# Attention row sums as four concurrent 32-column tiles, and the PSUM banks regrouped, in a beacon-attention plus GEGLU kernel

## The chip, the cores and the metric

The kernel runs on one core of one Trainium2 chip. The metric is the device time of one execution in microseconds (us). Every kernel was timed in several rounds beside the kernel before on the same chip, and fast runs are compared with fast runs. The profile that is quoted is one profiled execution. Its span runs from the first to the last instruction, and it is some 2 us shorter than the time.

Engines: PE is TensorE doing matmuls, PEld is TensorE loading weights, DVE is VectorE, ACT is ScalarE, POOL is GpSimd. PSUM is the memory that the matmuls of this program write to; the program cuts it into banks of 512 columns. The granted clock is TensorE's clock as a share of full speed.

A trace can lack a few per cent of the matmul records. "Start to start" is the time between the starts of two matmuls that follow each other.

## The reference

The sizes are batch 8, 8 heads, 576 queries, 576 + 16 keys (the "beacon" keys come first and everybody sees them), head dimension 64. The attention output, 4608 tokens of 512 values, goes through a GEGLU block with 1536 hidden values.

```python
k_all = np.concatenate([beacon_k, k], axis=2)          # 16 + 576 keys
v_all = np.concatenate([beacon_v, v], axis=2)
scores = scale * np.matmul(q, k_all.transpose(0, 1, 3, 2))
scores = np.where(causal, -1000000000.0, scores)       # beacons never masked
a = np.exp(scores - scores.max(-1, keepdims=True))
a /= a.sum(-1, keepdims=True) + 1e-09                  # the row sums of this case
x = np.matmul(a, v_all)                                # -> (4608, 512)
g = x @ w_gate
gelu = 0.5 * g * (1.0 + erf(g * inv_sqrt2))
return gelu * (x @ w_val) @ w_out
```

## The kernel before

The program goes through the eight batch entries. Each has an *attention stage* over four head pairs, called heads 0 to 3 here and in the prediction, and then a *gate stage* over 512 tokens. A head pair goes like this: scores on TensorE, exp on ScalarE (four instructions), masks (on GpSimd; in batch entry 0 on VectorE), then `attend`, which makes the value product X and the row sums Z, and `normalize`, which makes X/Z and writes it to `xT_sb`. Between them stand the out-projection matmuls of the token chunk before, the calls `o(n)`. They are the filler of the attention stage.

`attend` makes the row sums with a matrix of ones of 64 columns. One head of the pair lands in partitions 0 to 63, the other in 64 to 127, and each row sum is written 64 times over:

```python
for w, (ps, base, split) in enumerate(x_of[i]):        # w = 0: X, w = 1: Z
    for q0, q1 in ((S_LO[t], split), (max(split, S_LO[t]), S)):
        # ... (cut)
        for hi in range(2):
            mm(ps[64 * hi : 64 * hi + 64, base + q0 : base + q1],
               ones[0:kr, :] if w else v_sb[0:kr, t, 2 * m + hi, :],
               expT[0:kr, hi, e0 : e0 + q1 - q0], ...)
```

`normalize` does not take the reciprocal of all 128 x 576 copies. It transposes blocks of 32 x 32, takes the reciprocal of one column of each block, and transposes back with a broadcast. In batch entry 0 ScalarE does it with Ln and Exp instead (`by_act`).

```python
if by_act:
    act(ln_sb, z_ps, ACT.Ln)
    # ... (cut)
    act(rec_sb, ln_sb, ACT.Exp, scale=-1.0)
else:
    if not direct:
        act(x_sb, x_ps, ACT.Copy)
    keep(nc.vector.transpose(zT_sb, z_ps))
    keep(nc.vector.reciprocal(r_sb, zT_sb...[:, :, 0:1]))
    keep(nc.vector.transpose(rec_sb..., r_sb.to_broadcast([P, S // 32, 32])))
keep(nc.vector.tensor_tensor(out=xT_sb[:, m, b * S : (b + 1) * S], in0=x_sb, in1=rec_sb, op=ALU.mult))
```

The order of one batch entry, and of its first gate tile:

```python
o(6); ab(0); o(10); cd(0); o(8)        # ab, cd: scores and exps, two halves
for m in range(1, NPAIR):
    ab(m); av(m - 1); cd(m)            # av: attend and normalize
    o(6 if m < NPAIR - 1 else 5)
av(3, direct=True)
o(7)
for fi in range(F_TILES):
    gate_val(b, fi, kk_late=fi == 0)   # first tile: the two matmuls that need head 3 come last
    # ... (cut: after the first tile, GpSimd issues the loads of entry b + 2)
```

The eight matmuls of the first gate tile are sorted so that the seventh is the first that needs head 3. That *seventh gate matmul* is where an attention stage ends for TensorE, and most of this document is about it.

The softmax here doesn't subtract the row's maximum and nothing guards it: scores larger than these inputs give would overflow.

## Time and profile before

| before | |
|---|---|
| time, median of 3 fast runs | 398.17 us (397.83 to 398.93) |
| span of the profiled run | 396.2 us |
| TensorE busy | 382.3 us (97%) |
| seventh gate matmul after the last xT, all eight stages | 0.05 us |
| normalisation, first transpose to end of xT (29 of them) | 2.68 to 2.69 us |
| X and Z of one head pair on TensorE | 1.56 us |
| start of the last score matmul after the one before, entries 2 to 7 | 334 to 339 ns, against 204 ns without a wait |

The first line of the profile page's part 1 gives the busy time and share of each engine, and the first line of part 4 the chain of waits, shared out among the engines. Both say TensorE. The third line is from the list of waits: what waited for what, total us, times, longest.

```profile
PE 382.3 (97%) x3046; PEld 185.9 (47%) x3046; DVE 190.5 (48%) x304; ACT 202.2 (51%) x280; POOL 156.3 (39%) x277
...
PE 79%; DMA 8%; POOL 3%; DVE 3%; ACT 3%; issue 2%; SPq 2%; POOLq 0%; ACTq 0%
...
PE gv_ps L155 <- DVE xT_sb L312: 0.8, 1, 0.8
```

VectorE seems to be of no weight: busy 48%, 3% of the chain. The end of a stage shows something else. Here are the VectorE timeline of the kernel before at the end of batch entry 2, and under it the TensorE timeline at the same place. The columns are start, duration, engine, line, operation, tiles, shapes, count.

```profile
114.70 0.78 DVE L304 STREAM_TRANSPOSE zT_sb<-x_ps 128x576 f32<-128x576 f32 x1 [0.74 <-ACT x_sb L158]
115.52 0.27 DVE L305 RECIPROCAL r_sb<-zT_sb 128x18 f32<-128x18 f32 x1
115.82 0.78 DVE L307 STREAM_TRANSPOSE rec_sb<-r_sb 128x576 f32<-128x576 f32 x1
116.63 0.76 DVE L312 TENSOR_TENSOR xT_sb<-x_sb,rec_sb 128x576 bf16<-128x576 f32 x1
117.31 0.78 DVE L304 STREAM_TRANSPOSE zT_sb<-x_ps 128x576 f32<-128x576 f32 x1
118.12 0.27 DVE L305 RECIPROCAL r_sb<-zT_sb 128x18 f32<-128x18 f32 x1
118.42 0.78 DVE L307 STREAM_TRANSPOSE rec_sb<-r_sb 128x576 f32<-128x576 f32 x1
119.23 0.76 DVE L312 TENSOR_TENSOR xT_sb<-x_ps,rec_sb 128x576 bf16<-128x576 f32 x1
```

```profile
118.64 0.81 PE L155 MATMUL gv_ps<-xT_sb,wg_sb 128*128 128x512 bf16 x3
119.28 0.81 PE L155 MATMUL gv_ps<-xT_sb,wv_sb 128*128 128x512 bf16 x3
120.04 0.38 PE L155 MATMUL gv_ps<-xT_sb,wg_sb 128*128 128x512 bf16 x1
```

The chains of heads 2 and 3 stand one behind the other on VectorE without a gap. The last ends at 119.23 + 0.76 = 119.99, and the seventh gate matmul starts at 120.04. TensorE's starts are 216 ns apart there and this one comes 327 ns after the sixth: a wait of only 0.11 us. The program is tuned so that VectorE and TensorE arrive at the same moment. VectorE has no slack, and in entries 1 to 7 two whole normalisations of each stage lie on that path.

### The profile page before, as it was taken

How to read it: one execution, taken by the hardware profiler on the slowest of the kernel's cores; microseconds unless marked ns; L12 is line 12 of the kernel's file. 1: busy time of each engine (PE TensorE's matmuls, PEld its weight loads, DVE VectorE, ACT ScalarE, POOL GpSimd, SP SyncE). 2: the span in 40 equal slices, each digit the busy share in tenths (PEclk: the TensorE clock that was granted, in tenths of full speed). 3: DMA queues.
4: the chain of work that ended last, by engine and by line, in shares of the span. 5: the costliest groups of instructions: out<-in, count | busy, mean ns of one | idle time of the engine just before them, and what ended most of it. 6: DMA issues, size and time to landing. Idle time of an engine off the chain costs nothing.

```text
span 396.2 us, 7413 instructions
## 1 busy us (share of the span) xinstructions
PE 382.3 (97%) x3046; PEld 185.9 (47%) x3046; DVE 190.5 (48%) x304; ACT 202.2 (51%) x280; POOL 156.3 (39%) x277
## 2 busy tenths in 40 slices
PE   3889999999999999999999999999999999999996
PEld 2464545544454445444544455444544455444442
DVE  1393654844375327642673338433754266332332
ACT  2775258634873379336843586347823793332210
POOL 8722395780369124931486047803400240000000
PEclk9999999999999999999999999999999999999999
DMA  7999998699129930996099915991032010000012
GB/s 91 180 206 204 175 132 97 68 169 121 55 36 156 141 79 30 120 156 84 29 107 162 89 55 57 163 137 58 28 89 59 34 45 32 0 0 29 28 53 106
DMA packets 139154, 36.24 MB, mean 91 GB/s; under 512 B 126832, under 2 KB 134512, under 8 KB 139120
## 3 DMA queue, kind: packets, MB, share of 16 engines
q0 software_dynamic: 103984, 19.14, 64.4%
q1 hardware_dynamic: 35136, 16.62, 19.3%
q8 instruction: 24, 0.39, 0.4%
q14 instruction: 10, 0.08, 0.1%
HBM read 38.27 MB, written 9.44 MB: 120 GB/s over the span
## 4 chain that ended last, share of the span: by engine, by line
PE 79%; DMA 8%; POOL 3%; DVE 3%; ACT 3%; issue 2%; SPq 2%; POOLq 0%; ACTq 0%
PE gv_ps L155 36%; PE o_ps L155 23%; PE x_ps L155 11%; PE s_ps L155 8%; DMA qkT<-k_sb_94 3%; DMA v_sb_98<-in_beacon_v_dram 2%; SPq L196 2%; ACT expT L158 2%; DMA k_sb_97<-in_k_dram 2%; POOL k_sb_97 L109 1%; PE t_ps L167 1%; DVE qkT L178 1%; POOL q_sb_96 L109 1%; PE w_ps L155 1%; DMA kb<-in_beacon_k_dram 1%
## 5 line engine op out<-in xcount | busy, mean ns | idle before, releaser
L158 ACT ACTIVATE ge_sb<-gv_ps 128x512 bf16<-128x512 f32 x108 | 64.5, 597 | 150.7 <-PE gv_ps L155 150.7
L340 DVE TENSOR_TENSOR hT_sb<-gv_ps,ge_sb 128x512 bf16<-128x512 f32 x108 | 74.7, 692 | 116.0 <-ACT ge_sb L158 116.0
L158 ACT ACTIVATE expT<-s_ps 128x1024 bf16<-128x1024 f32 (+3 forms) x128 | 103.9, 870 | 25.8 <-PE s_ps L155 25.7
L155 PE MATMUL gv_ps<-xT_sb,wg_sb 128*128 128x512 bf16 x432 | 112.2, 379 | 0.8 <-DVE xT_sb L312 0.8
L155 PE MATMUL gv_ps<-xT_sb,wv_sb 128*128 128x512 bf16 x432 | 112.2, 379 | 0.0
L238 POOL TENSOR_SCALAR_AFFINE_SELECT expT<-expT 128x256 bf16<-128x256 bf16 (+2 forms) x140 | 52.4, 388 | 142.2 <-ACT expT L158 142.1
L155 PE MATMUL o_ps<-wo_sb,hT_sb 128*128 128x512 bf16 x432 | 103.6, 380 | 0.0
L155 PEld LDWEIGHTS <-wv_sb 128*128 128x128 bf16 x432 | 42.3, 98 | 52.7 <-issue 2.7
L155 PEld LDWEIGHTS <-wg_sb 128*128 128x128 bf16 x432 | 41.9, 98 | 49.9
L155 PEld LDWEIGHTS <-hT_sb 128*128 128x128 bf16 x432 | 38.8, 98 | 46.6 <-issue 2.8
L364 DVE COPY o_sb<-o_ps 128x512 f32<-128x512 f32 x36 | 24.7, 687 | 37.9 <-PE o_ps L155 37.9
L155 PE MATMUL s_ps<-qkT 64*128 64x80 bf16 (+5 forms) x384 | 39.1, 294 | 2.7 <-DVE qkT L183 1.5
L155 PE MATMUL x_ps<-expT,ones 128*64 128x432 bf16 (+1 forms) x558 | 41.2, 243 | 0.0
L304 DVE STREAM_TRANSPOSE zT_sb<-x_ps 128x576 f32<-128x576 f32 x29 | 22.7, 781 | 29.9 <-ACT x_sb L158 29.9
L155 PEld LDWEIGHTS <-qkT 64*128 64x128 bf16 x384 | 14.8, 96 | 30.4 <-issue 21.8
L155 PEld LDWEIGHTS <-ones 128*64 128x64 bf16 (+1 forms) x578 | 23.2, 110 | 4.6
L307 DVE STREAM_TRANSPOSE rec_sb<-r_sb 128x576 f32<-128x576 f32 x29 | 22.6, 778 | 1.0
L155 PE MATMUL x_ps<-expT,v_sb_95 128*64 128x80 bf16 (+5 forms) x270 | 21.5, 245 | 1.5 <-DVE zT_sb L304 1.1
L155 PE MATMUL x_ps<-expT,v_sb_98 128*64 128x80 bf16 (+5 forms) x288 | 22.8, 246 | 0.0
L109 POOL DMA_DIRECT2D v_sb_98<-in_v_dram x20 | 17.0, 868 | 11.9 <-DMA wv_sb<-in_moe_w_val_dram 3.7
L109 POOL DMA_DIRECT2D v_sb_95<-in_v_dram x20 | 17.0, 889 | 2.5 <-DMA k_sb_94<-in_k_dram 2.3
L312 DVE TENSOR_TENSOR xT_sb<-x_sb,rec_sb 128x576 bf16<-128x576 f32 x23 | 17.4, 758 | 0.9
(51 smaller groups left out, 190.9 us busy)
## 6 DMA issues: line engine op xcount, KB each, us to landing
out_dram<-o_sb SPq DMA_DIRECT2D x36, 256.0 KB, 2.0
v_sb_95<-in_v_dram POOLq DMA_DIRECT2D x12, 128.0 KB, 7.9
wg_sb<-in_moe_w_gate_dram POOLq DMA_DIRECT2D x3, 512.0 KB, 11.6
wv_sb<-in_moe_w_val_dram POOLq DMA_DIRECT2D x3, 512.0 KB, 13.3
wo_sb<-in_moe_w_out_dram POOLq DMA_DIRECT2D x1, 1536.0 KB, 23.5
v_sb_98<-in_v_dram POOLq DMA_DIRECT2D x12, 128.0 KB, 10.6
q_sb_93<-in_q_dram POOLq DMA_DIRECT2D x12, 128.0 KB, 4.2
q_sb_96<-in_q_dram POOLq DMA_DIRECT2D x12, 128.0 KB, 4.2
```

Source lines behind the costliest of these rows:

```text
L109: keep(nc.gpsimd.dma_start(out=out_ap, in_=in_ap))
L155: keep(nc.tensor.matmul(out_ap, lhsT, rhs, start=start, stop=stop, **kw))
L158: keep(nc.scalar.activation(out_ap, in_ap, func, **kw))
L167: keep(nc.tensor.transpose(out_ap, in_ap, ident[0:n, 0:n]))
L178: nc.vector.tensor_copy(qkT[:, m, :, NB:SK].rearrange("p w (t r) -> p w t r", r=6), t_ps[:, 0:2, 0:S].rearrange("p w (r t) -> p w t r", r=6),)
L196: nc.sync.dma_start_transpose(out=qkT[:, :, w, c + j * P : c + j * P + n], in_=src[0:n, j, :, :].rearrange("p h d -> p (h d)"),)
L238: nc.gpsimd.affine_select(out=d, in_=d, pattern=[[0, 2], [1, n]], compare_op=ALU.is_ge, fill=0.0, base=NB if t == 0 else 0, channel_multip ...
L304: keep(nc.vector.transpose(zT_sb, z_ps))
L307: nc.vector.transpose(rec_sb.rearrange("p (c o) -> p c o", o=32), r_sb.to_broadcast([P, S // 32, 32]))
L312: nc.vector.tensor_tensor(out=xT_sb[:, m, b * S : (b + 1) * S], in0=x_sb, in1=rec_sb, op=ALU.mult)
L340: nc.vector.tensor_tensor(out=h_of[ci][:, fi, :], in0=gv_ps[:, 1, :], in1=ge_sb, op=ALU.mult)
L364: keep(nc.vector.tensor_copy(o_sb[:, ti, :], o_ps))
```

## The change

The intent is to make the row sums cheaper on TensorE. A matrix of ones of only 32 columns is enough, and four such tiles can run at once where two of 64 columns ran before. So the queries of a head are split in two sets of nearly equal work: 0 to 159 and 448 to 575 in partitions 0 to 31 of the head, 160 to 447 in partitions 32 to 63. X and Z then need 1024 PSUM columns instead of 1536, and the bank that comes free becomes a second one for the out-projection.

There is a price in `normalize`. The transposed row sums of a set are only in its own 32 partitions, while every partition of the head needs all queries. So there are three reciprocals and, for each head of the pair, two small copies that exchange the two sets between the partition groups. In batch entry 0, moreover, `by_act` no longer means Ln and Exp: all four heads go through the VectorE chain, and `by_act` only moves the copy of X.

```diff
-            keep(nc.vector.transpose(zT_sb, z_ps))
-            keep(nc.vector.reciprocal(r_sb, zT_sb.rearrange("p (c o) -> p c o", o=32)[:, :, 0:1]))
+        keep(nc.vector.transpose(zT_sb, z_ps))                   # 288 columns, not 576
+        z = zT_sb.rearrange("p (c o) -> p c o", o=32)[:, :, 0:1]
+        n0, n1 = ZA // 32, ZB // 32
+        for c, zc, n in ((0, 0, n0), (n1, n0, S // 32 - n1), (n0, 0, n1 - n0)):
+            keep(nc.vector.reciprocal(r_sb[:, c : c + n, :], z[:, zc : zc + n, :]))
+        for a in (0, 64):
+            ra, rb = r_sb[a : a + 32], r_sb[a + 32 : a + 64]
+            keep(nc.vector.tensor_copy(ra[:, n0:n1, :], rb[:, n0:n1, :]))
+            keep(nc.vector.tensor_copy(outer(rb), outer(ra)))
 ... (cut: attend)
+        for t, g in Z_ORDER:
+            for lo, end, col in Z_GROUPS[g]:
+                ...
+                    p0 = 64 * hi + 32 * g
+                    mm(x_ps[p0 : p0 + 32, ...], ones[0 : KROWS[t], 0:32], expT[...], ...)
 ... (cut)
-    psum_o = ctx.enter_context(tc.tile_pool(name="psum_o", bufs=1, ...))
+    psum_o = ctx.enter_context(tc.tile_pool(name="psum_o", bufs=2, ...))
 ... (cut: batch entry 0)
-            av(1, by_act=True)
-            av(2, wide=True, by_act=True, direct=True)
-            av(3, by_act=True, direct=True)
+            av(1, psum_s, "s", by_act=True)
+            av(2)
+            av(3, psum_s, "s", direct=True)
```

More of the change, by code (lines that the diff above doesn't have):

```diff
@@ L38 @@
 AV_ORDER = [0, 2, 4, 1, 3]
-X0 = 16
-Z0 = X0 + S
+Z0 = S
+ZW = S // 2
+ZA, ZB = 160, 448
+Z_GROUPS = [[(0, ZA, 0), (ZB, S, ZA)], [(ZA, ZB, 0)]]
+Z_ORDER = [(0, 1), (0, 0), (1, 1), (1, 0), (2, 1), (2, 0), (3, 1), (3, 0), (4, 0)]
 QK_SCALE = 0.125
@@ L77 @@
     psum_x = ctx.enter_context(tc.tile_pool(name="psum_x", bufs=1, space=bass.MemoryType.PSUM))
-    psum_o = ctx.enter_context(tc.tile_pool(name="psum_o", bufs=1, space=bass.MemoryType.PSUM))
+    psum_o = ctx.enter_context(tc.tile_pool(name="psum_o", bufs=2, space=bass.MemoryType.PSUM))
     ident = const.tile([P, P], BF16, name="ident", tag="ident")
@@ L161, in transpose_pe @@
     def transpose_pe(b, m, pool, tag):
-        t_ps = pool.tile([P, 3 if tag == "x" else 2, 1024], BF16, name="t_ps", tag=tag)
+        t_ps = pool.tile([P, 2, 1024], BF16, name="t_ps", tag=tag)
         qk, kb = qk6[b]
@@ L251, with attend @@
     x_of = {}
-    def attend(b, m, t, wide=False):
+    def attend(b, m, pool, tag):
         i = b * NPAIR + m
-        if t == AV_ORDER[0]:
-            if wide:
-                x_of[i] = tuple(
-                    (psum_s.tile([P, 1024], FP32, name=name, tag="s"), 0, 512) for name in ("xs_ps", "zs_ps")
-                )
-            else:
-                x_ps = psum_x.tile([P, 1536], FP32, name="x_ps", tag="x")
-                x_of[i] = ((x_ps, X0, 512 - X0), (x_ps, Z0, 1024 - Z0))
+        x_of[i] = x_ps = pool.tile([P, 1024], FP32, name="x_ps", tag=tag)
         expT, v_sb = exp_of[i], v_ring[b % NRING]
-        kr, first, last = KROWS[t], t == AV_ORDER[0], t == AV_ORDER[-1]
-        for w, (ps, base, split) in enumerate(x_of[i]):
-            for q0, q1 in ((S_LO[t], split), (max(split, S_LO[t]), S)):
+        for t in AV_ORDER:
+            for q0, q1 in ((S_LO[t], 512), (512, S)):
                 if q0 >= q1:
@@ L271, in attend, with outer @@
                     mm(
-                        ps[64 * hi : 64 * hi + 64, base + q0 : base + q1],
-                        ones[0:kr, :] if w else v_sb[0:kr, t, 2 * m + hi, :],
-                        expT[0:kr, hi, e0 : e0 + q1 - q0],
-                        first and (wide or not (w == 1 and q0 == 0)),
-                        last,
+                        x_ps[64 * hi : 64 * hi + 64, q0:q1],
+                        v_sb[0 : KROWS[t], t, 2 * m + hi, :],
+                        expT[0 : KROWS[t], hi, e0 : e0 + q1 - q0],
+                        t == AV_ORDER[0],
+                        t == AV_ORDER[-1],
                         skip_group_check=True,
                     )
+        for t, g in Z_ORDER:
+            for lo, end, col in Z_GROUPS[g]:
+                q0 = max(lo, S_LO[t])
+                if q0 >= end:
+                    continue
+                e0 = EXP_OFF[t] + q0 - S_LO[t]
+                for hi in range(2):
+                    p0 = 64 * hi + 32 * g
+                    mm(
+                        x_ps[p0 : p0 + 32, Z0 + col + q0 - lo : Z0 + col + end - lo],
+                        ones[0 : KROWS[t], 0:32],
+                        expT[0 : KROWS[t], hi, e0 : e0 + end - q0],
+                        t == 0 and lo < ZB,
+                        t == (4 if g == 0 else 3),
+                        skip_group_check=True,
+                    )
+    def outer(r):
+        return r.rearrange("p (g c) o -> p g (c o)", c=13)[:, :, 0:5]
     def normalize(b, m, by_act=False, direct=False):
         i = b * NPAIR + m
-        (x_ps, xc, _), (z_ps, zc, _) = x_of.pop(i)
-        x_ps, z_ps = x_ps[:, xc : xc + S], z_ps[:, zc : zc + S]
+        xz_ps = x_of.pop(i)
+        x_ps, z_ps = xz_ps[:, 0:S], xz_ps[:, Z0 : Z0 + ZW]
         del exp_of[i]
-        rec_sb = npool.tile([P, S], FP32, name="rec_sb", tag="rec_sb")
         x_sb = x_ps
@@ L292, in normalize @@
             x_sb = npool.tile([P, S], FP32, name="x_sb", tag="x_sb")
-        if by_act:
-            ln_sb = npool.tile([P, S], FP32, name="ln_sb", tag="zT_sb")
-            act(ln_sb, z_ps, ACT.Ln)
-            if not direct:
+            if by_act:
                 keep(nc.vector.tensor_copy(x_sb, x_ps))
-            act(rec_sb, ln_sb, ACT.Exp, scale=-1.0)
-        else:
-            zT_sb = npool.tile([P, S], FP32, name="zT_sb", tag="zT_sb")
-            r_sb = npool.tile([P, S // 32, 1], FP32, name="r_sb", tag="r_sb")
-            if not direct:
-                act(x_sb, x_ps, ACT.Copy)
-            keep(nc.vector.transpose(zT_sb, z_ps))
-            keep(nc.vector.reciprocal(r_sb, zT_sb.rearrange("p (c o) -> p c o", o=32)[:, :, 0:1]))
-            keep(
-                nc.vector.transpose(
-                    rec_sb.rearrange("p (c o) -> p c o", o=32), r_sb.to_broadcast([P, S // 32, 32])
-                )
+            else:
+                act(x_sb, x_ps, ACT.Copy)
+        rec_sb = npool.tile([P, S], FP32, name="rec_sb", tag="rec_sb")
+        zT_sb = npool.tile([P, ZW], FP32, name="zT_sb", tag="zT_sb")
+        r_sb = npool.tile([P, 26, 1], FP32, name="r_sb", tag="r_sb")
+        keep(nc.vector.transpose(zT_sb, z_ps))
[7 more added lines that the diff above has]
+            keep(nc.vector.tensor_copy(outer(rb), outer(ra)))
+        keep(
+            nc.vector.transpose(
+                rec_sb.rearrange("p (c o) -> p c o", o=32), r_sb[:, 0 : S // 32, :].to_broadcast([P, S // 32, 32])
             )
+        )
         keep(
@@ L343, in gate_val, with out_mms @@
         )
-    def out_mms(ci, u0, u1, wide=lambda ti: False):
+    def out_mms(ci, u0, u1):
         for u in range(u0, u1):
@@ L350, in out_mms @@
             if fi == 0:
-                if wide(ti):
-                    o_of[ci][1] = psum_x.tile([P, 1536], FP32, name="o_ps", tag="x")[:, 0:D_MODEL]
-                else:
-                    o_of[ci][1] = psum_o.tile([P, D_MODEL], FP32, name="o_ps", tag="o")
+                o_of[ci][1] = psum_o.tile([P, D_MODEL], FP32, name="o_ps", tag="o")
             o_sb, o_ps = o_of[ci]
@@ L394, in o @@
             if b:
-                out_mms(b - 1, u[0], u[0] + n, lambda ti: ti == 0)
+                out_mms(b - 1, u[0], u[0] + n)
                 u[0] += n
@@ L404, in cd, with av @@
             scores(b, m, 3)
-        def av(m, wide=False, **kw):
-            for t in AV_ORDER:
-                attend(b, m, t, wide)
+        def av(m, pool=psum_x, tag="x", **kw):
+            attend(b, m, pool, tag)
             normalize(b, m, **kw)
@@ L461 @@
         gate_val(N_CHUNKS - 1, fi)
-        out_mms(N_CHUNKS - 2, 4 * fi, 4 * fi + 4, lambda ti: ti % 2 == 0)
-    out_mms(N_CHUNKS - 1, 0, 4 * F_TILES, lambda ti: ti % 2 == 0)
+        out_mms(N_CHUNKS - 2, 4 * fi, 4 * fi + 4)
+    out_mms(N_CHUNKS - 1, 0, 4 * F_TILES)
 _INS = ['q', 'k', 'v', 'beacon_k', 'beacon_v', 'moe_w_gate', 'moe_w_val', 'moe_w_out']
```

## The prediction

> **What bounds the kernel now.** TensorE is busy 97% of the span (page, part 1), but the timeline of an attention stage (batch entry 2, 97.4 to 118.6 us) shows more.
>
> 1. Inside a head pair ScalarE sets the pace. The second exp ends 2.38 us after the first score matmul, and the last score matmul waits for it: it starts 334 ns after the one before, against 204 ns where nothing holds it. The 1.56 us of value and row-sum matmuls lie inside that window, with some 0.13 us of slack.
> 2. At the stage's end VectorE sets the pace. The normalisations of heads 2 and 3 run one behind the other, 2.61 us each (start to start: transpose 0.82, reciprocal 0.30, transpose 0.81, multiply 0.68). In all eight stages the seventh gate matmul starts 0.05 us after the last xT is written (here 120.04 after 119.99).
> 3. In batch entry 0 ScalarE makes reciprocals by Ln and Exp, so VectorE does little; the gate goes on at 31.95 us.
>
> **What changes.** Row sums: 18 matmuls in two tiles (1664 columns each, about 0.72 us) become 22 in four. In-order issue over groups of 800 and 864 columns gives about 0.42 us, estimated at the trace's 2.4 columns per ns. The Trainium skill, TensorEngine Tiling, Key Properties, says that a change of tiling mode drains the array; here such changes cost about 0.10 us, and one is added. Attention saves 0.15 to 0.2 us per head pair. By point 1 nearly all of it turns into waiting for exps; after head 3, into waiting for VectorE. The second out-projection bank removes no wait that I find.
>
> VectorE, per head pair: the first transpose falls from 0.82 to about 0.52 us. One reciprocal becomes three (+0.13), and four small copies come in, partly chained (+0.67). A small copy here takes 156 ns, and a dependent instruction starts about 35 ns after its predecessor's end. The skill's VectorE: DVE Perf Modes (errata section) measures a fixed cost of about 150 cycles per instruction, which agrees. Net +0.5 us (0.35 to 0.7): a normalisation of 3.1 us.
>
> **On the critical path.** Batch entries 1 to 7: two serial normalisations, +1.0 us each, 7.0 us in all. Batch entry 0: heads 0 to 3 all go through the VectorE chain: from 23.7 us, 3.1 + 0.9 (masks) + 0.7 + 3 x 3.1 puts the last xT near 37.8 us, 5.9 us later. TensorE stands nearly idle there for some 8 us. The clock then drops, as at 14.7 us, where warm-up matmuls start 450 ns apart against 216 later; I add 2 us.
>
> 398.2 + 7.0 + 5.9 + 2 = **413 us**; range **406.5 to 418**. Chances: faster by over 2%: 0.02; within 2%: 0.10; slower by over 2%: 0.88.
>
> **What would show each step.** Row sums: span near 0.42 us per head pair, the last score matmul's gap near 0.5 us. Normalisation: 3.1 us from first transpose to next instruction. Seventh gate matmul: still just after xT; idle before it up from 0.1 to about 1.2 us in entries 1 to 7; near 37.8 us in entry 0, with gate matmuls just after at 430 ns.
>
> **What would make it wrong.** Small VectorE instructions overlapping or costing 70 ns: then about 404. ScalarE waits that shrink after all. A clock that stays up in entry 0: 411. A four-tile stream that serialises would be mostly hidden.

## The result, and the profile after

The changed kernel takes 421.59 us, 5.8% longer. Ratios here are the mean time of one kernel's fast runs over that of the other's of the same rounds, so they are not quite the ratios of the medians. This one is 1.058 (95% interval 1.055 to 1.060). The result is correct. It lies above the predicted range of 406.5 to 418 us.

The profiled run of that first measurement took 555.03 us. It was slow, with a mean granted clock of 0.662 where the three other runs had 0.984 to 0.988, so it is used for nothing here but one count. The kernel was therefore run again:

> The changed kernel once more, to have its profile in the fast state: the one that came with the result ran at a granted clock of 0.66 and took 555 us. Both theories: about 421 us in the fast state. Port theory: in the profile, the small copies that overlap no GpSimd instruction take about 163 ns, those that overlap one up to about 600 ns and end with it; a normalisation takes about 3.17 us undisturbed and 3.6 to 4.0 us in a stage with masks and DMA issues; the seventh gate matmul follows the last xT by 0.05 us in every stage, with about 2 us of idle time before it. Rival (clock): normalisations take 3.17 us everywhere, and the missing 8 us is matmuls that start 430 ns apart at a low clock.

It took 420.33 us (419.87 to 421.71), ratio 1.056, and its profile is a fast one, with a span of 419.7 us. All readings of the kernel after are from this profile. The same three lines, and then the clock of part 2 (40 equal slices, tenths of full speed):

```profile
PE 377.1 (90%) x3183; PEld 179.7 (43%) x3234; DVE 221.0 (53%) x505; ACT 198.8 (47%) x275; POOL 157.3 (37%) x277
...
PE 64%; DVE 23%; ACT 9%; issue 2%; DMA 1%; POOL 0%; ACTq 0%; POOLq 0%
...
PE gv_ps L160 <- DVE xT_sb L331: 20.3, 10, 2.6
...
PEclk9995999989999999999999999999999999999999
```

TensorE is busy 5 us less (by records of which some are missing) and the whole takes 23.5 us more. VectorE's share of the chain went from 3% to 23%, and gate matmuls wait for xT for 20.3 us in all, up from 0.8. The clock falls at two places: at 31.0 to 41.3 us (batch entry 0) and at 89.1 to 92.5 us (entry 1).

The end of entry 2 on VectorE (head 2's small copies, then all of head 3's chain), then on GpSimd and on TensorE:

```profile
127.57 0.22 DVE L322 COPY r_sb<-r_sb 32x9 f32<-32x9 f32 x1
127.83 0.38 DVE L324 COPY r_sb<-r_sb 32x10 f32<-32x10 f32 x1
128.22 0.17 DVE L322 COPY r_sb<-r_sb 32x9 f32<-32x9 f32 x1
128.42 0.17 DVE L324 COPY r_sb<-r_sb 32x10 f32<-32x10 f32 x1
...
130.11 0.48 DVE L315 STREAM_TRANSPOSE zT_sb<-x_ps 128x288 f32<-128x288 f32 x1
130.62 0.35 DVE L319 RECIPROCAL r_sb<-zT_sb 128x5 f32<-128x5 f32 x3
131.00 0.16 DVE L322 COPY r_sb<-r_sb 32x9 f32<-32x9 f32 x1
131.20 0.58 DVE L324 COPY r_sb<-r_sb 32x10 f32<-32x10 f32 x1
131.79 0.17 DVE L322 COPY r_sb<-r_sb 32x9 f32<-32x9 f32 x1
131.99 0.47 DVE L324 COPY r_sb<-r_sb 32x10 f32<-32x10 f32 x1
132.50 0.78 DVE L326 STREAM_TRANSPOSE rec_sb<-r_sb 128x576 f32<-128x576 f32 x1
133.31 0.76 DVE L331 TENSOR_TENSOR xT_sb<-x_ps,rec_sb 128x576 bf16<-128x576 f32 x1
```

```profile
127.37 0.81 POOL L243 TENSOR_SCALAR_AFFINE_SELECT expT<-expT 128x256 bf16<-128x256 bf16 x2 [0.66 <-ACT expT L163]
128.26 4.21 POOL L114 DMA_DIRECT2D q_sb<-in_q_dram  x5
```

```profile
131.10 0.81 PE L160 MATMUL gv_ps<-xT_sb,wv_sb 128*128 128x512 bf16 x3
134.13 0.38 PE L160 MATMUL gv_ps<-xT_sb,wg_sb 128*128 128x512 bf16 x1 [2.22 <-DVE xT_sb L331]
```

The seventh gate matmul still starts 0.05 us after xT, but now 2.60 us after the sixth matmul. Two things lengthened the chain. It has more instructions, as the diff says. And some of the copies of 9 or 10 elements take 0.16 us, others 0.38, 0.47 or 0.58. The long ones have company on GpSimd: the copy at 127.83 ends at 128.21, with the masks (127.37 + 0.81 = 128.18). Of the five DMA issues of the second line, the single records put the end of the fourth at 131.785 and of the fifth at 132.470. The copy of 131.20 ends at 131.78 and that of 131.99 at 132.46.

Counted over the whole fast profile, 52 of the 128 copies took over 200 ns (none lies between 169 and 219), and every one of them overlapped a GpSimd instruction: 40 a mask, 11 a DMA issue, one both. 56 copies overlapped no GpSimd instruction, and not one of them was long. 20 overlapped one (19 a DMA issue, one the last 0.13 us of a mask) and were not. (In the slow profile: 53 long, and again none of the undisturbed ones.) Over the undisturbed 165 ns the copies took 11.8 us in all.

The 19 are set apart by their start. They started before the DMA issue or at most 0.16 us after its start; the 11 held up by a DMA issue alone started at least 0.24 us after. In the fast profile of e4 below, copies that started up to 0.16 us after were not held and those from 0.25 us on were, but for one that touched the last 1 ns of an issue. So in these two traces a DMA issue holds the copies only from some point between 0.16 and 0.24 us after its start.

Two batch entries make a control within the same profile. In entries 6 and 7 nothing is left to load, so no DMA issue stands beside head 3. There head 3's normalisation, from first transpose to the end of xT, took 3.23 us; in entries 2 to 5 it took 3.96 to 3.97. The wait before the seventh gate matmul, start to start, was 2.60 to 2.67 us in entries 1 to 5, and 1.87 us in entries 6 and 7.

TensorE did get its saving in heads 0 to 2. X and Z of a head pair take 1.35 us there, down from 1.56. But in entries 2 to 7 the last score matmul now starts 550 ns after the one before, up from 339. (Score matmuls come in pairs, one for each head of the head pair, so this is the distance of the last two pairs.) The 0.21 us saved became 0.21 us of waiting for the exp. TensorE's timeline before head 3, first before (one line of two pairs), then after:

```profile
113.84 0.60 PE L155 MATMUL s_ps<-qkT 64*128 64x464 bf16 x4
```

```profile
125.42 0.37 PE L160 MATMUL s_ps<-qkT 64*128 64x464 bf16 x2
125.97 0.27 PE L160 MATMUL s_ps<-qkT 64*128 64x208 bf16 x2 [0.18 <-ACT expT L163]
```

In head 3 nothing was saved: its X and Z take 1.58 us, since the last value matmuls start only at 128.24, just after GpSimd's last mask ends (128.18). Before, the row sums stood between the value matmuls and filled that time.

And batch entry 0 loses 7.8 us: its seventh gate matmul starts at 38.25 us and the gate stage of entry 1 at 84.22 us, before at 31.95 and 76.44. First before, then after:

```profile
31.95 0.38 PE L155 MATMUL gv_ps<-xT_sb,wg_sb 128*128 128x512 bf16 x1 [0.84 <-DVE xT_sb L312]
```

```profile
35.10 0.58 PE L160 MATMUL gv_ps<-xT_sb,wg_sb 128*128 128x512 bf16 x1 [2.56 <-DVE xT_sb L331]
35.91 1.06 PE L160 MATMUL gv_ps<-xT_sb,wv_sb 128*128 128x512 bf16 x2 [0.22 <-issue]
38.25 0.59 PE L160 MATMUL gv_ps<-xT_sb,wg_sb 128*128 128x512 bf16 x1 [1.28 <-DVE xT_sb L331]
38.63 0.64 PE L160 MATMUL gv_ps<-xT_sb,wv_sb 128*128 128x512 bf16 x1
```

### The profile page after: what moved, and what is told of

Same layout as the page of the kernel before. It is cut to its first block, busy times and chain, and to the rows that moved or that the text cites. A ratio compares the mean times of both kernels' runs of the same rounds, so it can differ in the third digit from the quotient of the medians.

```text
span 553.1 us, 7980 instructions
## 1 busy us (share of the span) xinstructions
PE 533.3 (96%) x3234; PEld 209.6 (38%) x3234; DVE 223.3 (40%) x505; ACT 201.1 (36%) x275; POOL 160.1 (29%) x277
## 4 chain that ended last, share of the span: by engine, by line
PE 88%; DVE 8%; DMA 1%; ACT 1%; issue 1%; POOL 1%; POOLq 0%
PE gv_ps L160 50%; PE o_ps L160 23%; PE x_ps L160 8%; PE s_ps L160 6%; DVE rec_sb L326 2%; DVE xT_sb L331 2%; DVE r_sb L324 1%; DMA qk_103<-in_k_dram 1%; DVE r_sb L322 1%; DVE zT_sb L315 1%; PE t_ps L172 1%; DVE r_sb L319 1%; PE w_ps L160 1%; ACT x_sb L163 1%; POOL qk_103 L114 1%
## 5 line engine op out<-in xcount | busy, mean ns | idle before, releaser
L160 PE MATMUL gv_ps<-xT_sb,wg_sb 128*128 128x512 bf16 x432 | 162.8, 511 | 7.3 <-DVE xT_sb L331 7.3
L160 PE MATMUL gv_ps<-xT_sb,wv_sb 128*128 128x512 bf16 x432 | 164.0, 517 | 0.0
L160 PE MATMUL o_ps<-wo_sb,hT_sb 128*128 128x512 bf16 x432 | 148.6, 501 | 0.0
L160 PEld LDWEIGHTS <-wv_sb 128*128 128x128 bf16 x432 | 52.8, 122 | 95.8 <-issue 95.8
L160 PEld LDWEIGHTS <-wg_sb 128*128 128x128 bf16 x432 | 51.0, 119 | 90.0 <-issue 89.2
L160 PEld LDWEIGHTS <-hT_sb 128*128 128x128 bf16 x432 | 46.3, 115 | 79.6 <-issue 75.9
L315 DVE STREAM_TRANSPOSE zT_sb<-x_ps 128x288 f32<-128x288 f32 x32 | 15.4, 481 | 30.7 <-ACT x_sb L163 30.7
L160 PE MATMUL x_ps<-expT,v_sb_95 128*64 128x64 bf16 (+6 forms) x320 | 19.5, 275 | 1.1 <-ACT expT L163 1.1
L160 PE MATMUL x_ps<-expT,ones 128*32 128x128 bf16 (+6 forms) x704 | 20.0, 253 | 0.0
L160 PE MATMUL x_ps<-expT,v_sb_98 128*64 128x64 bf16 (+6 forms) x320 | 19.4, 274 | 0.0
L324 DVE COPY r_sb<-r_sb 32x10 f32<-32x10 f32 x64 | 18.5, 289 | 2.2
```

Of the source, the lines that this page charges most:

```text
L160: keep(nc.tensor.matmul(out_ap, lhsT, rhs, start=start, stop=stop, **kw))
L324: keep(nc.vector.tensor_copy(outer(rb), outer(ra)))
```

## The experiments

All kernels below give a correct result. "e1" and so on are versions of the kernel after unless the text says otherwise. The time of the kernel before beside them was 397.86 to 398.62 us.

| kernel | us, median | ratio to before (95%) |
|---|---|---|
| after, again | 420.33 | 1.056 (1.054 to 1.059) |
| e1 copies by another operation | 412.83 | 1.037 (1.034 to 1.040) |
| e4 before, with the added VectorE work only | 420.96 | 1.056 (1.051 to 1.060) |
| e6 e1, and entry 0 by ScalarE again | 405.84 | 1.020 (1.018 to 1.022) |
| e10 e6, one matmul as filler, head 3 as before | 401.00 | 1.007 (1.005 to 1.009) |
| e13 e1, row sums made twice | 417.00 | 1.047 (1.044 to 1.050) |
| e14 e1, row sums made slower by a little over the saving | 413.53 | 1.037 (1.034 to 1.040) |
| e8 e1, one out-projection bank | 413.15 | 1.037 (1.035 to 1.039) |
| e5 e1, the two sets one behind the other | 412.94 | 1.037 (1.035 to 1.039) |
| e2 two gate tiles begun before the wait | 420.57 | 1.057 (1.053 to 1.061) |
| e7 e6, other order at head 2 | 408.35 | 1.025 (1.023 to 1.027) |
| e9 e6, one matmul as filler | 404.50 | 1.015 (1.012 to 1.017) |
| e11 before, one matmul moved | 431.43 | 1.083 (1.081 to 1.085) |
| e12 e10, two matmuls moved | 403.99 | 1.014 (1.012 to 1.016) |

**The theories.** Theory A: VectorE's chain decides, and it is longer than predicted because its small copies wait for a port to SBUF that GpSimd holds. Theory B: the chain decides, but the copies are slow by themselves or by their number. Theory C: the loss comes from elsewhere, from TensorE's new tiling or the new PSUM tiles.

The Trainium skill gives theory A its mechanism (page "SBUF — State Buffer", section "Who interferes with whom"). VectorE and GpSimd share one pair of ports as an exclusive lock. A copy can enter a mode that uses the pair, and the loser "fully blocks" until the other's instruction is over. `tensor_reduce` on trn2 never contends. The trace agrees: each of the 52 long copies ends within 0.03 us of the end of a GpSimd instruction. e1 tests it.

### e1: the same copies by an operation that needs no shared port

```diff
+    def moved(out_ap, in_ap):   # maximum over one element: a copy
+        ...
+        keep(nc.vector.tensor_reduce(out=out_ap, in_=in_ap, op=ALU.max, axis=mybir.AxisListType.X))
-            keep(nc.vector.tensor_copy(ra[:, n0:n1, :], rb[:, n0:n1, :]))
-            keep(nc.vector.tensor_copy(outer(rb), outer(ra)))
+            moved(ra[:, n0:n1, :], rb[:, n0:n1, :])
+            moved(outer(rb), outer(ra))
```

> The four small copies of each normalisation become four reductions over one element (same partitions, same bytes, same order)[...]. Port theory: each takes some 160 ns whatever GpSimd does, a normalisation is about 3.2 us in all stages, and the kernel gains 5 to 7 us on the changed one: about 415 us. Rival (the loss is the number of small instructions, or the clock): within 1 us of the changed kernel.

It took 412.83 us, 7.5 us less than the kernel after. The groups by shape, which end in busy us, mean ns of one, and idle time before them, show it: first the kernel after, then e1.

```profile
L324 DVE COPY r_sb<-r_sb 32x10 f32<-32x10 f32 x64 | 18.4, 287 | 2.2
...
L322 DVE COPY r_sb<-r_sb 32x9 f32<-32x9 f32 x64 | 14.5, 227 | 1.5
```

```profile
L302 DVE TENSOR_REDUCE r_sb<-r_sb 32x10 f32<-32x10 f32 x64 | 9.9, 155 | 2.2
L302 DVE TENSOR_REDUCE r_sb<-r_sb 32x9 f32<-32x9 f32 x64 | 9.8, 154 | 1.5
```

The same number of instructions on the same bytes takes 155 ns instead of 227 and 287, although 108 of the 128 overlap a GpSimd instruction. All 32 normalisations now take 3.19 to 3.21 us, where the kernel after had 3.23 to 3.97 (mean 3.61). The wait before the seventh gate matmul is 1.34 us, start to start, in each of entries 1 to 7. (By itself the new operation is some 10 ns faster than an undisturbed copy, 3.20 us instead of 3.23 for a normalisation: 14 x 0.03 = 0.4 of the 7.5 us, an estimate.) The clock no longer drops in entry 1; in entry 0 it still does. TensorE's timeline of e1 at the end of entry 2:

```profile
128.13 0.81 PE L160 MATMUL gv_ps<-xT_sb,wv_sb 128*128 128x512 bf16 x3
129.90 0.38 PE L160 MATMUL gv_ps<-xT_sb,wg_sb 128*128 128x512 bf16 x1 [0.96 <-DVE xT_sb L334]
```

Theory B falls as the reason for the surprise, since neither number nor size changed. Theory A holds.

### e4: only the VectorE work, in the kernel before

```diff
-            keep(nc.vector.reciprocal(r_sb, zT_sb...[:, :, 0:1]))
+            for c, n in ((0, 5), (14, 4), (5, 9)):
+                keep(nc.vector.reciprocal(r_sb[:, c : c + n, :], z[:, c : c + n, :]))
+            for a in (0, 64):
+                ra, rb = r_sb[a : a + 32], r_sb[a + 32 : a + 64]
+                keep(nc.vector.tensor_copy(ra[:, 5:14, :], rb[:, 5:14, :]))
+                keep(nc.vector.tensor_copy(outer(rb), outer(ra)))
```

> The kernel before, with only the small VectorE instructions of the change put into its normalisation (three reciprocals for one, four copies that copy equal values); matmuls, PSUM and batch entry 0's Ln and Exp stay as before. VectorE theory: a normalisation grows from 2.61 to about 3.5 us undisturbed (the long transpose stays) and to 3.9 to 4.3 with GpSimd beside it, twice per stage on the critical path: +2.2 to 3 us in each of batch entries 1 to 7, so 414 to 419 us. If these instructions were not what costs, it stays within 2 us of 398.

Here TensorE's tiling, the PSUM tiles and entry 0 are those of the kernel before, and the copies move values that are equal anyway. It took 420.96 us, a little more than expected. Its normalisations take 3.54 us where GpSimd is quiet and 3.70 to 4.09 us elsewhere, and a stage takes 44.2 us (the last) to 46.7 us, mostly 45.0, up from 42.2. The two longest stages are those with 3.4 us at half clock, after the 2.5 us waits of entries 2 and 5. A few small VectorE instructions alone cost as much as the whole change, though for another sum: here the transpose is not halved, and entry 0 is nearly spared (its seventh gate matmul comes 1.2 us later). Theory C is not needed.

### e6: batch entry 0 by ScalarE again

```diff
+    def av_wide(b, m):     # 64-column row sums, X and Z in two score tiles
+        ...
+        act(ln_sb, zs[:, 0:S], ACT.Ln)
+        act(rec_sb, ln_sb, ACT.Exp, scale=-1.0)
+        ...
-            av(1, psum_s, "s", by_act=True)
+            av_wide(0, 1)
             av(2)
-            av(3, psum_s, "s", direct=True)
+            av_wide(0, 3)
```

> The one-port kernel, with heads 1 and 3 of batch entry 0 as in the kernel before: 64-column row sums and reciprocals by Ln and Exp on ScalarE, each in two score tiles of PSUM. VectorE then has two chains there instead of four. If the serial chains of batch entry 0 and the half clock after them are worth 7.8 us as the traces say, the seventh gate matmul comes at about 33 us instead of 38.6, no half clock is recorded there, and the kernel takes about 405.5 us. If entry 0 is not a cause: 412.8.

On top of e1, two of the four heads of entry 0 get their reciprocals from ScalarE as before. The time fell by 7.0 us to 405.84 us. The seventh gate matmul of entry 0 starts at 33.11 us, and the clock stays up throughout. This is entry 0's part by experiment; the trace of the kernel after had said 7.8 us.

What remains over the kernel before is 7.4 us. Some 1.2 us of it is still entry 0 (33.11 us against 31.95). The rest should be the two chains of each stage, each 3.20 us instead of 2.69: 7 stages x 2 x 0.52 us (from the unrounded durations) = 7.3 us. Together these estimates are 1.1 us more than was measured. e10 tests half of the chains' part.

### e9 and e10: filler into the new wait, and head 3 with the old chain

```diff
                 av(m - 1)
+                o(1)
                 cd(m)
-                o(6 if m < NPAIR - 1 else 5)
+                o(5 if m < NPAIR - 1 else 4)
```

> e6 with one out-projection matmul per head pair moved into the window in which TensorE waits for ScalarE (between the row sums and the second half of the scores). The gap before the last score matmul is 550 ns there against 204 ns with no wait, so 0.35 us of waiting can take one matmul of 0.216 us and one more change of tiling mode of 0.10 us. If the saving of the four-tile row sums is really sitting in that gap, 3 x 0.216 us comes back in each of seven stages: 405.8 - 4.5 = 401.3 us. If the gap is not idle TensorE time, no gain.

> e9 with head 3 of entries 1 to 7 as in the kernel before on VectorE and TensorE (64-column row sums, one reciprocal, no copies), in two score tiles of PSUM. If the two serial normalisations bound the stage's end, the last goes from 3.13 to 2.61 us: 0.5 us in each of seven stages, 401.3 - 3.6 = 397.7 us, just under the kernel before. If it is the matmuls that count, it loses 7 x 0.3 us instead.

e9 puts one out-projection matmul where TensorE waits for the exp. The wait was filled (the last score matmul now starts 206 ns after the one before), but the time fell only 1.3 us, to 404.50 us, where 401.3 was expected. Heads 1 and 2, and 2 and 3, followed each other after 3.98 and 3.81 us instead of 4.03 (by their last score matmuls, entries 2 to 7), heads 0 and 1 after 4.44 as before. So the three matmuls moved shortened a stage by 0.27 us and not by 0.65. That ScalarE sets the pace again is the likely reason, not a tested one.

e10 adds to e9 that head 3 of each stage gets its row sums in 64 columns, in PSUM tiles of its own, and the old chain of VectorE. One filler matmul also goes from behind head 3 to before it:

```diff
-                o(5 if m < NPAIR - 1 else 4)
-            av(3, direct=True)
-            o(7)
+                o(5)
+            av_wide(b, 3)       # transpose 576, one reciprocal, transpose, multiply
+            o(6)
```

It took 401.00 us, 3.5 us less, as expected (3.6). Head 3's normalisation took 2.68 us again, and the wait before the seventh gate matmul fell from 1.34 to 0.83 us, start to start:

```profile
121.48 0.38 PE L160 MATMUL gv_ps<-xT_sb,wg_sb 128*128 128x512 bf16 x1 [0.45 <-DVE xT_sb L376]
```

Head 3's four-tile row sums were given up and the kernel became faster, which is a direct sign of who sets the pace at the end of a stage. (The matmuls given back cost no time that the traces show: X and Z of head 3 take 2.01 us in e10 and 2.02 in e9.) This is the best version found, 0.7% above the kernel before: within 2% of it, not better.

### e13 and e14: is TensorE's saving really hidden?

```diff
-        for t, g in Z_ORDER:
+        for t, g in Z_ORDER * 2:                  # e13, all row sums twice
+        for t, g in Z_ORDER[:2] * 2 + Z_ORDER:    # e14, the two steps of the first key tile twice more
```

> The one-port kernel with all row-sum matmuls done twice (the second pass starts the sums anew, so the result is right): 22 more matmuls, about 0.36 us of TensorE time per head pair. If this time is hidden behind ScalarE (heads 0 to 2, where 0.35 us of waiting stands before the last score matmul) and behind VectorE (head 3, 1.1 us of waiting), the kernel stays within 1.5 us of 412.8 and the gap before the last score matmul falls from 550 to about 205 ns. If TensorE time counts there: 28 x 0.36 = 10 us more, about 423.

> The one-port kernel with the row sums of the first key tile done three times (each pass starts the sums anew, so the result is right): about 0.24 us more TensorE time per head pair, which gives back what the change saved (0.21 us) and a little more, but less than the 0.35 us that stand before the last score matmul. If what the change saved is hidden there: within 1 us of 412.8 us, and the gap before the last score matmul at about 310 ns. If TensorE time counts: 28 x 0.24 = 6.7 us more, about 419.5.

Both stand on e1, with its 412.83 us. In e13 the row sums take 0.37 us more in each head pair, and 28 head pairs in the seven stages would make 28 x 0.37 = 10.4 us if nothing were hidden. It cost 4.2 us. That is a mixed answer, because 0.37 us is more than the wait holds: the last score matmul stands at 207 ns, the wait is used up, and ScalarE's copy of X comes 0.13 to 0.26 us later after the exp before it. (In e13's profile TensorE also waits 1.3 us for a transposing DMA of q in one stage, in e1's 0.5 us, so the row sums' part of the 4.2 us is smaller still.) e14 therefore adds 0.245 us, a little over the 0.21 us that the change saves. Not hidden, that would be 28 x 0.245 = 6.9 us; it cost 0.7 us (413.53 against 412.83, whose ranges overlap), and in entries 2 to 7 the last score matmul still had some wait left (304 ns). So making the row sums slower by more than the change made them faster changes almost nothing. The saving is hidden, as predicted.

### e8: the second out-projection bank

```diff
-    psum_o = ctx.enter_context(tc.tile_pool(name="psum_o", bufs=2, ...))
+    psum_o = ctx.enter_context(tc.tile_pool(name="psum_o", bufs=1, ...))
+                if wide(ti):     # as in the kernel before: some tiles borrow the attention tile
+                    o_of[ci][1] = psum_x.tile([P, 1024], FP32, name="o_ps", tag="x")[:, 0:D_MODEL]
```

> The one-port kernel with the out-projection in PSUM as in the kernel before: one bank of its own, and the attention tile's for every first (in the tail every second) tile. No trace shows a wait for an out-projection bank, so within 1 us of 412.8. If the second bank was worth anything, slower by more than that.

413.15 us against e1's 412.83, with overlapping ranges: the second bank is worth nothing that can be seen in this program order.

### e11: the kernel before with one matmul moved

The idea was to use the 0.11 us that the kernel before has left. One out-projection matmul goes from before head 3's attention to behind it.

```diff
-                o(6 if m < NPAIR - 1 else 5)
+                o(6 if m == 1 else 5)
             av(3, direct=True)
-            o(7)
+            o(8)
```

> The kernel before with one out-projection matmul moved from between heads 2 and 3 to behind head 3, where TensorE waits 0.11 us for VectorE. Chain theory: the wait goes, 7 x 0.1 = 0.7 us, about 397.6 us. Rival: 398.4.

It took 431.43 us, 33 us more. The move pushed the last matmul of the third out-projection tile behind a place where VectorE is busy. The fourth tile's first matmul needs the only bank, which is free once VectorE has copied the third tile out, and that copy now stands behind a normalisation. TensorE's timeline of e11 shows it:

```profile
75.65 1.86 PE L155 MATMUL o_ps<-wo_sb,hT_sb 128*128 128x512 bf16 x4 [3.73 <-DVE o_sb L364]
```

That comes seven times, 3.7 us each, and six of the waits are followed by half clock, five times for 3.4 us and once for 6.8. So a second bank may be worth something after all: not time, but freedom in placing the filler (the same move with two banks was not run). The kernel before had paid for its one bank with a placement in which this wait does not occur.

### e2: two gate tiles begun before the wait

If TensorE waits for xT, it could do the first six matmuls of the *second* gate tile meanwhile.

```diff
+            if fi == 0:
+                gate_val(b, 0, 0)      # all but the matmuls that need head 3
+                gate_val(b, 1, 0)
+            gate_val(b, fi, 1 if fi < 2 else None)
```

> The changed kernel, with the matmuls of the first two gate tiles that need head 3 moved behind all twelve that do not: TensorE then has 2.6 us of work instead of 1.3 us before it needs the last normalisation. If the loss is TensorE waiting for VectorE's serial normalisations at the end of each stage, each of eight stages gets 1.3 us back: about 411 us. If the loss lies elsewhere (row-sum matmuls, clock, out-projection banks), the time stays at about 421 us.

It took 420.57 us against 420.33: nothing gained. TensorE's timeline of e2 at the same place:

```profile
133.57 0.38 PE L160 MATMUL gv_ps<-xT_sb,wg_sb 128*128 128x512 bf16 x1 [0.62 <-DVE xT_sb L331]
...
135.57 1.02 PE L160 MATMUL gv_ps<-xT_sb,wg_sb 128*128 128x512 bf16 x4 [0.98 <-DVE hT_sb L364]
```

The wait for xT shrank to less than 1 us, as intended. But now both PSUM tiles for scores and gates are held until xT comes, so the third gate tile has to wait for the gelu and the multiply of the first. A stage took 44.0 us instead of 44.5, and entry 0 lost 1.6 us by the same order. The wait had moved from a value to a buffer.

### e5: the two sets one behind the other

```diff
-Z_ORDER = [(0, 1), (0, 0), (1, 1), (1, 0), (2, 1), (2, 0), (3, 1), (3, 0), (4, 0)]
+Z_ORDER = [(t, 1) for t in range(4)] + [(t, 0) for t in range(5)]
```

> The one-port kernel, with the row-sum matmuls of one query set all before those of the other, so that only two of the four tiles run at a time: the row sums take about 0.7 us instead of 0.38 us per head pair. If TensorE time between the scores is hidden behind ScalarE, and head 3's behind VectorE, the kernel stays within 1.5 us of the one-port kernel (412.8), and the gap before the last score matmul falls from 550 to about 220 ns. If TensorE bounds these stages it loses 28 x 0.33 = 9 us: about 422.

This was meant to make the row sums run two at a time and so to take the saving away. It failed as an experiment: the row sums took 358 ns from first to last start instead of 347. The trace shows why. The program's source gives the widths 288, 288, 288, 288, 208, 208, 80, 80, 160, 160, 128 and so on; the records start them in the order 288, 288, 160, 160, 128, 128, 288, 288. The matmuls of the second set, whose tiles were free, started before matmuls that stand ahead of them in the source (the order of the compiled instructions was not looked at). The time of 412.94 us therefore says nothing about hiding, and e13 and e14 took its place.

### e7 and e12: more filler at the end of a stage

```diff
-                o(6 if m < NPAIR - 1 else 5)     # e7, on e6
+                o(5)
             av(3, direct=True)
-            o(7)
+            o(9)
-                o(5)                             # e12, on e10
+                o(4 if m < NPAIR - 1 else 5)
             av_wide(b, 3)
-            o(6)
+            o(8)
```

> e6 with two more moves at the end of the stages of entries 1 to 7: VectorE's transpose of head 2's row sums comes before ScalarE's copy of the same tile instead of after it (VectorE starts some 0.8 us earlier), and two out-projection matmuls move from between the heads to behind head 3 (0.43 us more work while VectorE finishes). By the chain theory about 1.1 us less waiting in each of seven stages: about 397 to 399 us. If the end of the stage is not what counts, it stays at e6.

> e10 with two out-projection matmuls of each stage moved from between the heads to behind head 3, where TensorE still waits 0.61 us for the last normalisation. Chain theory: the heads follow one another 0.2 us sooner, and the wait falls to about 0.2 us: 7 x 0.43 = 3 us, 401.0 - 3.0 = 398 us, level with the kernel before. If VectorE or ScalarE can't go faster between the heads: 401.

Both miss, and both lost what they meant to gain. In e7 the wait before the seventh gate matmul did go (0.37 us start to start, from 1.34). But head 2's first transpose also goes ahead of ScalarE's copy of X. VectorE was still busy with the chain of head 1, so ScalarE's copy waited for VectorE, the exps came later, and so did the masks. TensorE's timeline of e7 shows head 3's attention waiting twice for GpSimd:

```profile
118.84 0.39 PE L160 MATMUL x_ps<-expT,v_sb 128*64 128x400 bf16 x4 [0.62 <-POOL expT L243]
119.84 0.28 PE L160 MATMUL x_ps<-expT,v_sb 128*64 128x144 bf16 x4 [0.62 <-POOL expT L243]
```

That took 408.35 us, against e6's 405.84. In e12 the move made VectorE's copy of an out-projection tile ready just between the two chains of the stage. It takes 0.60 us of VectorE there, and the wait before the seventh gate matmul did not shrink: 403.99 us, against e10's 401.00.

## Why the prediction was wrong

It named the right mechanism and missed the size of one term. Point by point:

- *"Inside a head pair ScalarE sets the pace"; the saving turns into waiting.* Right. X and Z fell by 0.21 us in each of heads 0 to 2 (predicted 0.15 to 0.2) and the wait for the exp rose by 0.21 us; in head 3 the saving went into a wait for a mask, which the prediction did not have; the last score matmul stands at 550 ns (predicted near 500). e14 shows that the saving is hidden. The row sums took about 0.38 us, predicted 0.42.
- *"At the stage's end VectorE sets the pace."* Right. The seventh gate matmul still starts 0.05 us after xT in all eight stages; e1, e4, e6 and e10 all move the time by shortening or lengthening this chain.
- *"The second out-projection bank removes no wait that I find."* Right in this order (e8). e11 shows what it could have been good for.
- *Batch entry 0, 5.9 + 2 us.* Right in the sum: 7.8 us by the trace, 7.0 us by e6. The last xT came at 38.20 us (predicted near 37.8), the seventh gate matmul 6.3 us later than before (38.25), and 1.5 us more came after it. The gate matmuls stood 427 ns apart there, predicted 430. (The warm-up matmuls at 14.7 us from which that was taken stand 402 to 427 ns apart in the trace, not 450.) The Trainium skill ("TensorE: Matmul & The Clock Gate", Part 1) says that the clock falls to half after an idle window of some 3.4 us. The trace, with 10.2 us at 0.5, agrees in the half clock; but of the 3.4 us before the fall at 31.0 us TensorE was idle for only 2.3, counted from the matmul records.
- *"Four small copies come in, partly chained (+0.67)... Net +0.5 us (0.35 to 0.7): a normalisation of 3.1 us."* **This is the step that failed.** An undisturbed normalisation took 3.16 us from the first transpose to the next instruction, so the count and the single durations were about right. The term was sized from instructions that nothing disturbed. The copies stand beside GpSimd's masks and DMA issues, and 52 of 128 were held up, the longest to 0.58 us. The normalisations took 3.23 to 3.97 us to the end of xT, 3.61 us in the mean, against 2.69 us before: +0.92 instead of +0.5.
- *"Batch entries 1 to 7: ... +1.0 us each, 7.0 us in all."* Wrong by the same step: the span grew by 23.5 - 7.8 = 15.7 us there. The wait before the seventh gate matmul became 2.60 to 2.67 us, start to start, in five stages and 1.87 us in two. With the port contention taken away (e1) it is 1.34 us, 1.02 us above the 0.32 us of before, which is the predicted 1.0. In entry 1 the longer wait was also followed by 3.4 us at half clock. That is some 1.7 us, an estimate from the clock record; e1, with the shorter wait, has none there. It is probably not in every run: the seven fast runs of the kernel after have a mean clock of 0.984 (three) or 0.987 to 0.988 (four), and the three are 1.3 us longer in the mean.

The 22 us by experiment: 7.5 us are the port contention and what follows from it (after to e1), 7.0 us are batch entry 0 (e1 to e6), and 7.4 us are left between e6 and before. Of this rest, e10 gave back 3.5 us with one of the two chains alone; that the other half is the second chain and some of entry 0 is an estimate from their durations and was not tried. Had the 7.5 us not been there, 412.8 us would have met the 413.0 us predicted.

Why the clock fell after the wait of entry 1 and not after the nearly equal waits of entries 2 to 5 can be read from the clock record. All its changes lie whole multiples of 3.41 us apart (31.04, 41.28, 89.07 and 92.48 us). In the stretch of that length that ends at 89.07, TensorE was idle for 2.3 us, counted from the matmul records: nearly the whole wait of entry 1 fell into it. The waits of entries 2 to 5 were cut in two by an edge of these stretches, and none of the stretches there was idle for more than 1.7 us. In e4 the clock fell at the end of two stretches with 2.3 us idle, and not where a wait left 1.9 us or less in a stretch. So in these two traces the fall depends on how a wait lies to these edges; that rests on a few cases.

Two things stay open: why a DMA issue of GpSimd's does not hold the copies from its start; and what put the first profiled run into the slow state.

## What to carry to other kernels

Before you trade work of a busy engine for work of an idle one, look at which instruction the next stage waits for: a busy share of 97% and a chain share of 3% for VectorE hid that two of its chains ended every stage, so every 0.5 us added to a chain came back 14 times. Size an added instruction in the company it will have, not alone: a copy of ten elements cost 0.16 us by itself and up to 0.58 us beside GpSimd, and an operation that does not use the shared port (here a maximum over one element) gave that back at no cost. When you fill a wait, check first which buffers the filler holds and which engine must free them (e2, e11, e12).

## What the Trainium skill lacked or had wrong

- "SBUF — State Buffer", "Who interferes with whom": the rule agrees (52 long copies, all of them beside GpSimd; `tensor_reduce` 155 ns throughout). It gives no size for a small blocked copy: here 165 ns became as much as 0.58 us. It also does not say when a DMA issue of GpSimd's holds the port. Here 11 copies beside a DMA issue alone were held up (started 0.24 us or more after the issue's start) and 19 were not (at most 0.16 us after it).
- "TensorE: Matmul & The Clock Gate", Part 3: it says that matmuls are "pc-monotone in start AND end — strict FIFO, no reordering". In e5 the records start matmuls of free 32-column tiles ahead of earlier ones (288, 288, 160, 160, 128, 128, 288, 288, where the program's source has 288, 288, 288, 288, 208, 208, 80, 80, 160, 160, 128).
- The same page, Part 1: it puts the loss of the clock at idle windows of some 3.4 us. Here a gap of 2.67 us between starts in entry 1 was followed by 3.4 us at half clock, while gaps of 2.60 us in entries 2 to 5 were not: 2.3 us idle in one stretch of 3.41 us was enough, 1.7 us was not. Gaps below the stated length are no guarantee.
- "TensorEngine Tiling (Array Packing)", "Key Properties": it says that a change of tiling mode drains the array, but gives no duration. The trace of before shows about 0.10 us.
- "VectorE: DVE Perf Modes", the errata section: nothing lacking. Its fixed cost of about 150 cycles agrees with the undisturbed copies of 9 and 10 elements (165 ns, which at the page's 0.96 GHz is 158 cycles).
- No page that I read tells of a single core that runs a whole execution at a granted clock of about 0.66, as the run of 555.03 us did.
